# Attention ahead of two expert stages: keys and queries transposed head by head as loaded, with the sorting done while PSUM is emptied

## Chip, cores, metric

One core of one Trainium2 chip runs the whole program. The metric is the device time of one execution in microseconds; the kernel before took 967.55 us (median of three runs, 962.85 to 968.58).

## What is computed

The reference runs three stages in turn. Chunked attention: 8 batches, 8 heads, 576 positions, head width 64; each chunk of 64 positions attends to itself alone. Its output is read as 4608 rows (tokens) of 512 for two mixture-of-experts stages, each with 8 experts of which a row uses one.

```python
q_c = q.reshape(B, H, nc, chunk, D)                     # likewise k_c, v_c; chunk = 64
scores = scale * np.matmul(q_c, k_c.transpose(0, 1, 2, 4, 3))
scores = scores - np.max(scores, axis=-1, keepdims=True)
attn = np.exp(scores)
attn = attn / (np.sum(attn, axis=-1, keepdims=True) + 1e-09)
out = np.matmul(attn, v_c)                              # -> x of 4608 x 512
logits = x @ w_gate + modality_bias[modality_id]        # first expert stage; the second is alike
e_idx = np.argmax(logits, axis=1)
out[mask] = gate_w[mask, None] * (np.maximum(x[mask] @ w1[e], 0.0) @ w2[e])
```

## The kernel before

The attention runs over 36 tiles of 128 tokens. Two tiles are a unit: 256 tokens of all 8 heads, whose keys and queries are loaded together (`load_qk`, L434 to L443). Partition p of a loaded buffer holds the tokens 2p and 2p + 1 of each head, so that a run in memory is 512 bytes; heads lie outermost, then the token's parity r, then the 64 columns.

`reorder` (L452 to L460) copies such a buffer so that parity is outermost and two heads stand side by side. Units 0 to 2 are reordered by VectorE, units 3 to 17 by GpSimd, at L742 to L744. `emit_T` (L462 to L482) then makes one piece: four TensorE transposes of 128x128, for two head pairs and two parities, into one PSUM bank (tile `ps_t`, three buffers, shared with `ps_x`). A query piece is emptied by one ScalarE copy of 128x512 into `Tq` (L475), which puts even and odd tokens back in order by writing every second column. A key piece is emptied by two copies of 64x512 (L479), one for each head of the pairs, into `kb`, where the other head's half is blank so that one product serves two heads. A unit has four pieces (`pieces`, L484): keys and queries of the first two head pairs in its even slot, those of the last two in its odd slot.

The loop at L727 runs over the tiles; one turn t is a slot. Every engine works through its own queue in the order in which the slot names the work. TensorE's order is: scores of tile t + 2 (`emit_sc`, L497), first piece (keys, unit t // 2 + 2), transposes of the probabilities of tile t + 1 (`emit_pT`, L523), in each fourth slot the gate's products for four tiles (`emit_lg1`, L563), transposes of the output rows of tile t - 1 (`emit_xT`, L557), second piece (queries), products with the values of tile t (`emit_av`, L532). ScalarE empties the first piece, then `pt` (L525), in each fourth slot `lsb` (L567), `xT` (L558), the second piece, and runs exp for tile t + 2 (L515). VectorE takes the maximum and the difference of the scores (L506, L509) and normalises the output (L542 to L548).

Between these steps `drip()` calls one further step of `route` (L569), which chooses the expert of each row from the gate's products: small VectorE operations, the rank products (`ranks_mm`, L251 to L255), then four scatters into a table in device memory from GpSimd (L603). `wait2` is the number of calls that it lets pass ahead of the rank products. Three calls lie between the scores and the first piece.

Loads of keys, queries and values, stores and table blankings are all issued by SP, in program order. The table blankings are `tables` (L167), called from the list `g.late`, of which each slot takes three entries: in slot 2. From slot 20 on, `jobs` load the weights of the largest expert and split them (L637, L640). After the last tile the expert stages follow, which the change does not touch.

Of the kernel before, what the change touches and what calls it, by code (L numbers as in the profile page):

```python
# [134 lines left out]
def setup_late(nc, g, tmp, modality_id, modality_bias, w_gate2, w_skip):  # L135

    NT, NTILE, DM = g.NT, g.NTILE, g.DM
    md = tmp.tile([NTILE, P, 2], I32, name="md")
    nc.gpsimd.dma_start(
        out=md, in_=modality_id.bitcast(I32).rearrange("(t p w) -> t p w", p=P, w=2)  # L140
    )
    b01 = tmp.tile([P, 2, E], F32, name="b01")
    nc.gpsimd.dma_start(
        out=b01.rearrange("p m e -> p (m e)"),
        in_=modality_bias.rearrange("m e -> (m e)").unsqueeze(0).to_broadcast([P, 2 * E]),
    )
    wsm = tmp.tile([P, 4, E + 1], F32, name="wsm")
    nc.gpsimd.dma_start(out=wsm[:, :, 0:E], in_=w_gate2.rearrange("(a p) e -> p a e", p=P))
    nc.gpsimd.dma_start(
        out=wsm[:, :, E:E + 1], in_=w_skip.rearrange("(a p o) -> p a o", p=P, o=1)  # L150
    )


    blank = tmp.tile([P, g.NR // P, 2], I32, name="blank")
    nc.gpsimd.memset(blank[:, :, 0], int(OOB))
    nc.gpsimd.memset(blank[:, :, 1], 0)


    n = g.NR // P
    m = next(i for i in range(10, 0, -1) if n % i == 0)  # L160
    blank0 = tmp.tile([P, n // m, 16], I32, name="blank0")
    nc.gpsimd.memset(blank0, 0)
    nc.gpsimd.memset(blank0[:, :, 0], int(OOB))
    for t in g.row4:
        nc.gpsimd.memset(t, 0)

    def tables():  # L167
        nc.sync.dma_start(
            out=g.tab[0].rearrange("(p m n) c -> p m (n c)", p=P, m=m),
            in_=blank0.rearrange("p n c -> p (n c)").unsqueeze(1).to_broadcast([P, m, n // m * 16]),  # L170
        )
        nc.sync.dma_start(out=g.tab[1].rearrange("(p n) c -> p n c", p=P), in_=blank)

    nop = lambda: None

    mf = tmp.tile([NTILE, P], F32, name="mf")

    def bias():
        pm = g.ps_l.tile([P, P], F32, tag="l", name="pm")
        nc.tensor.transpose(pm[:, 0:NTILE], mf, g.ident[0:NTILE, 0:NTILE])  # L180
        m = tmp.tile([P, NTILE, 2], F32, name="m")
        nc.vector.tensor_copy(m[:, :, 1], pm[:, 0:NTILE])
        nc.vector.tensor_scalar(
            out=m[:, :, 0], in0=m[:, :, 1], scalar1=-1.0, scalar2=1.0, op0=ALU.mult, op1=ALU.add
        )
        t0 = tmp.tile([P, NTILE, E], F32, name="t0")
        sh = [P, NTILE, E]
        for i, dst in ((0, t0), (1, g.bias)):
            nc.vector.tensor_tensor(
                out=dst,  # L190
                in0=m[:, :, i:i + 1].to_broadcast(sh),
                in1=b01[:, i:i + 1, :].to_broadcast(sh),
                op=ALU.mult,
            )
        nc.vector.tensor_tensor(out=g.bias, in0=g.bias, in1=t0, op=ALU.add)

    def rows():

        pr = g.ps_l.tile([P, DM], F32, tag="l", name="pr")
        for a in range(4):  # L200
            nc.tensor.transpose(pr[0:E + 1, a * P:(a + 1) * P], wsm[:, a, :], g.ident)
        rw = tmp.tile([E + 1, DM], F32, name="rw")
        nc.scalar.copy(rw, pr[0:E + 1, :])
        nc.scalar.dma_start(out=g.rows, in_=rw)

    g.late = [lambda: nc.vector.tensor_copy(mf, md[:, :, 0])] + g.late + [tables, nop, bias, nop, nop, nop, rows]


def gate_argmax(nc, g, pool, lg, n, gate_out, comp=None):
# [178 lines left out]
def attention(ctx, tc, g, q, k, v, w_gate, w1, out, small):  # L388
# [11 lines left out]
    scale = 1.0 / float(D) ** 0.5  # L400
    ident = g.ident

    raw_p = ctx.enter_context(tc.tile_pool(name="raw", bufs=2))
    re_p = ctx.enter_context(tc.tile_pool(name="re", bufs=2))
    qt_p = ctx.enter_context(tc.tile_pool(name="qt", bufs=2))
    st_p = ctx.enter_context(tc.tile_pool(name="st", bufs=1))
    v_p = ctx.enter_context(tc.tile_pool(name="vp", bufs=1))
# [11 lines left out]
    kb = [v_p.tile([P, NA, 2, 4 * CH], F32, name=f"kb{i}") for i in range(2)]  # L419
    wg = g.const.tile([P, NA, 32], F32, name="wg")  # L420
    stage = [st_p.tile([P, 1024], F32, name=f"stage{i}") for i in range(2)]
    zero = g.zero[:, 0:1].unsqueeze(2).unsqueeze(3).to_broadcast([P, H, 2, D])

    def runs(t0, n):
        done = 0
# [3 lines left out]
            yield done, step, b, s  # L429
            done += step  # L430

    raw, re, T_ = {}, {}, {}

    def load_qk(u, queues=(nc.sync, nc.sync), parts=1):  # L434
        for src, nm, queue in ((k, "k", queues[0]), (q, "q", queues[1])):
# [13 lines left out]
            in_=v[b, h, c0 * CH:c1 * CH, :].rearrange("(c s) d -> s c d", s=CH),  # L449
        )  # L450

    def reorder(u, nm, eng, hs=slice(0, H)):  # L452
        t = raw[nm, u]
        if hs.start == 0:
            re[nm, u] = re_p.tile([P, 2, H, D], F32, tag="r" + nm, name="r" + nm)
        t2 = re[nm, u].rearrange("p r h d -> p h r d")
        if eng is nc.vector:
            eng.tensor_copy(t2[:, hs], t[:, hs])
        else:
            eng.tensor_tensor(out=t2, in0=t, in1=zero, op=ALU.add)  # L460

    def emit_T(u, nm, ah):  # L462
        t = re[nm, u]
        ps = ps_t.tile([P, 2, 2, P], F32, tag="t", name="ps_t")
        for a in range(2):
            for r in range(2):
                h = 2 * (2 * ah + a)
                nc.tensor.transpose(  # L468
                    ps[:, a, r, :], t[:, r, h:h + 2, :].rearrange("p h d -> p (h d)"), ident
                )  # L470
        sl = slice(2 * ah, 2 * ah + 2)
        if nm == "q":
            if ah == 0:
                T_[u] = qt_p.tile([P, NA, 4 * CH], F32, tag="Tq", name="Tq")
            nc.scalar.copy(T_[u][:, sl, :].rearrange("p a (c r) -> p a r c", r=2), ps)  # L475
        else:
            for j in range(2):
                eng = nc.vector.tensor_copy if u == 0 and j == 1 else nc.scalar.copy
                eng(  # L479
                    kb[u % 2][64 * j:64 * j + 64, sl, j, :].rearrange("p a (c r) -> p a r c", r=2),  # L480
                    ps[64 * j:64 * j + 64],
                )  # L482

    def pieces(u):  # L484
        return [lambda nm=nm, ah=ah: emit_T(u, nm, ah) for ah in range(2) for nm in ("k", "q")]
# [80 lines left out]
            )  # L566
        nc.scalar.copy(g.lsb, ps)  # L567

    def route(gi, wait=3, wait2=1):  # L569
        for _ in range(wait):  # L570
            yield
        ps = ps_l.tile([P, 4, NA, 32], F32, tag="l", name="ps_l2")
# [124 lines left out]
    ps = ps_t.tile([P, NA, P], F32, tag="t", name="ps_w")  # L697
    for i in range(15):
        nc.tensor.transpose(ps[:, i % NA, :], ident, ident)
    for i in range(2):  # L700
        for nm in "kq":
            reorder(0, nm, nc.vector, slice(i * H // 2, (i + 1) * H // 2))
    for f in pieces(0):
        f()
    reorder(1, "k", nc.vector)
    reorder(1, "q", nc.vector)
    T = pieces(1)
    emit_sc(0)
    emit_softmax(0)
# [11 lines left out]
    nc.gpsimd.dma_start(out=wg[:, :, 0:E], in_=w_gate.rearrange("(a p) e -> p a e", p=P))  # L721
    setup_late(nc, g, st_p, *small)
    load_qk(3)
    reorder(2, "k", nc.vector)
    reorder(2, "q", nc.vector)
    vq = []
    for t in range(NTILE):  # L727
        u = t // 2
# [8 lines left out]
        if t % 2 == 0:  # L737
            if u + 4 < NU:
                load_qk(u + 4)
            if u + 2 < NU:  # L740
                T = pieces(u + 2)
            for nm in "kq":  # L742
                if u + 3 < NU:
                    reorder(u + 3, nm, nc.gpsimd)  # L744
        if t >= 5 and (t - 5) % 4 == 0:
            store((t - 5) // 4)
        if t == NTILE - 3:
            nc.sync.dma_start(
                out=g.v0[:, 0:(E + 1) * DM],
                in_=g.rows.rearrange("e d -> (e d)").unsqueeze(0).to_broadcast([P, (E + 1) * DM]),  # L750
            )
# [738 lines left out]
```

## Time and profile before

| | us |
|---|---|
| median of three runs | 967.55 |
| lowest, highest | 962.85, 968.58 |
| the profiled execution | 963.45 |
| its span, first to last instruction | 961.8 |
| mean granted TensorE clock over the span | 0.985 |
| TensorE busy (matmuls) | 916.2 |
| VectorE, ScalarE, GpSimd busy | 648.6, 364.1, 321.8 |
| attention, to the end of its last product | 197.15 |

The profile is of one execution. A time in a timeline is counted from the span's start. A duration in a row is that of one instruction from its start to its end; where instructions overlap in an engine's pipeline, the next may start before that. In brackets stands how long the engine was idle before an instruction and what ended that.

### The profile page before, as it was taken

The numbers are of one execution on the slowest core, as the hardware profiler recorded it, in microseconds if no ns is written. First come the engines' busy times: TensorE is split into PE (matmuls) and PEld (weight loads), VectorE is DVE, ScalarE is ACT, GpSimd is POOL, SyncE is SP. The second block draws the span as 40 slices with busy tenths as digits, with TensorE's granted clock in tenths as the row PEclk, the third lists the DMA queues.
The fourth block names the chain that finished last, engine by engine and source line by source line (L and its number), as shares of the span: only waits on it lengthen the run. The fifth ranks groups of instructions, "written<-read, shape, count | busy, mean of one in ns | idle before, by whom it ended". The sixth has DMA issues, their size and how long they took to land. (4 is left out here: it accounts for less than half of the span.)

```text
span 961.8 us, 19826 instructions
## 1 busy us (share of the span) xinstructions
PE 916.2 (95%) x6757; PEld 812.0 (84%) x6757; DVE 648.6 (67%) x1853; ACT 364.1 (38%) x643; POOL 321.8 (33%) x288
## 2 busy tenths in 40 slices
PE   7889898999999999999999999999989997999996
PEld 6668777789999999989789999989879996998995
DVE  6567777678777777997887787787266265625261
ACT  5767686742222222522512222233145154515150
POOL 6447556434232323232232224212313121313310
PEclk9999998999999999999999999999999999999998
DMA  9999999757111111331111117000645366512400
GB/s 191 234 264 269 226 239 200 222 183 244 45 47 47 57 46 47 121 119 54 36 48 52 52 46 255 27 24 23 221 136 207 122 215 217 189 46 88 170 18 17
DMA packets 123292, 121.73 MB, mean 127 GB/s; under 512 B 55757, under 2 KB 94525, under 8 KB 122946
## 3 DMA queue, kind: packets, MB, share of 16 engines
q1 hardware_dynamic: 107536, 84.29, 32.5%
q0 software_dynamic: 14464, 34.43, 10.7%
q8 instruction: 83, 1.36, 0.7%
q14 instruction: 135, 1.11, 0.4%
q10 hardware_dynamic: 1074, 0.54, 0.2%
HBM read 96.37 MB, written 28.72 MB: 130 GB/s over the span
## 5 line engine op out<-in xcount | busy, mean ns | idle before, releaser
L1131 PE MATMUL p<-w2s,hT 128*128 128x512 f32 x1392 | 327.0, 392 | 0.2 <-DVEq L1246 0.2
L1131 PEld LDWEIGHTS p<-w2s,hT 128*128 128x128 f32 x1392 | 257.6, 188 | 51.5 <-DVEq L1246 0.6
L379 PE MATMUL p<-xTb,w1s 128*128 128x256 f32 x2064 | 262.0, 286 | 6.4 <-DVE hT L1096 3.0
L379 PEld LDWEIGHTS p<-xTb,w1s 128*128 128x128 f32 x2064 | 254.6, 192 | 11.1 <-DVE hT L1096 3.4
L1044 DVE CUSTOM_DVE_ANT_0 x<-x,v 128x512 f32<-128x512 f32 x333 | 210.5, 687 | 40.1 <-ACT x L1027 33.9
L1034 POOL DMA_INDIRECT out_dram<-x,ids x54 | 74.4, 1377 | 251.4 <-DVE x L1030 187.0
L1095 ACT ACTIVATE hT<-p 128x512 fp32r<-128x512 f32 x86 | 51.5, 599 | 194.6 <-PE p L379 169.9
L283 POOL DMA_INDIRECT tab<-rowP,posi x38 | 39.3, 1033 | 221.3 <-DVE idsP L1154 159.2
L1096 DVE SCALAR_TENSOR_TENSOR hT<-p,hT 128x512 fp32r<-128x512 f32 x86 | 58.9, 688 | 67.3 <-ACT hT L1095 44.7
L379 PE MATMUL p1t<-xTb,w1s 128*128 128x256 f32 x696 | 88.1, 283 | 0.0
L379 PEld LDWEIGHTS p1t<-xTb,w1s 128*128 128x128 f32 x696 | 85.1, 191 | 0.8 <-issue 0.8
L349 POOL DMA_INDIRECT x<-out_dram,ids x66 | 73.0, 1106 | 36.9 <-issue 17.3
L1027 ACT ACTIVATE x<-p,ids 128x512 f32<-128x512 f32 x33 | 22.7, 688 | 138.4 <-PE p L1131 130.8
L479 ACT COPY kb<-ps_t 64x512 f32<-64x512 f32 x70 | 43.9, 627 | 45.7 <-PE ps_t L468 45.3
L603 POOL DMA_INDIRECT tab<-row,posi x36 | 36.9, 1025 | 49.9 <-DVE x L548 24.2
L365 DVE TENSOR_TENSOR xTb<-px,xTb 128x512 fp32r<-128x512 f32 x70 | 44.8, 682 | 12.0 <-ACT xTb L364 12.0
L1004 DVE TENSOR_TENSOR w2s<-r,w2s 128x512 fp32r<-128x512 f32 x80 | 51.1, 688 | 1.2 <-ACT w2s L1002 0.8
L1002 ACT CAST w2s<-r 128x512 fp32r<-128x512 f32 x80 | 46.5, 625 | 8.1 <-issue 6.1
L364 ACT CAST xTb<-px 128x512 fp32r<-128x512 f32 x70 | 37.4, 591 | 27.6 <-PE px L362 27.6
L497 PE MATMUL sc<-kb,Tq 128*64 128x128 f32 x576 | 41.3, 284 | 5.8 <-DVE r_d L218 2.9
L1030 DVE SCALAR_TENSOR_TENSOR x<-p,ids,x 128x512 f32<-128x512 f32 x21 | 15.7, 749 | 44.2 <-PE p L1131 44.2
L497 PEld LDWEIGHTS sc<-kb,Tq 128*64 128x64 f32 x576 | 33.1, 141 | 10.4 <-issue 4.2
(229 smaller groups left out, 1102.4 us busy)
## 6 DMA issues: line engine op xcount, KB each, us to landing
r<-in_moe_w_dram SPq DMA_DIRECT2D x14, 2048.0 KB, 11.0
r<-in_moe_w_dram SPq DMA_DIRECT2D x20, 512.0 KB, 5.3
out_dram<-x SPq DMA_DIRECT2D x9, 1024.0 KB, 7.3
k<-in_k_dram SPq DMA_DIRECT2D x11, 512.0 KB, 6.4
q<-in_q_dram SPq DMA_DIRECT2D x11, 512.0 KB, 8.5
vt<-in_v_dram SPq DMA_DIRECT2D x32, 144.0 KB, 6.2
r<-in_moe_w_dram POOLq DMA_DIRECT2D x2, 2048.0 KB
v<-in_v_dram SPq DMA_DIRECT2D x24, 144.0 KB, 6.4
```

Of the source, the lines that this page charges most:

```text
L349: return [nc.gpsimd.indirect_dma_start(out=x[:, h, :], out_offset=None, in_=src, in_offset=IOff(ap=ids[:, h, 0:1], axis=0), bounds_check=s ...
L365: nc.vector.tensor_tensor(out=t[:, 1, :, h * P:(h + 1) * P], in0=ps, in1=o.bitcast(F32), op=ALU.subtract)
L379: nc.tensor.matmul(ps, w1s[:, b, kk, f * P:(f + 1) * P], xt[:, a, kk, :], start=(i == 0), stop=(i == 3 * KD - 1),)
L479: eng(kb[u % 2][64 * j:64 * j + 64, sl, j, :].rearrange("p a (c r) -> p a r c", r=2), ps[64 * j:64 * j + 64],)
L497: nc.tensor.matmul(out=ps[64 * c:64 * c + 64, a, :, :], lhsT=T_[u][:, a, cs], rhs=kb[u % 2][:, a, :, cs], start=True, stop=True,)
L1002: hi(s[:, 0, kk, :], r[:, kk, :])
L1004: eng.tensor_tensor(out=s[:, 1, kk, :], in0=r[:, kk, :], in1=s[:, 0, kk, :].bitcast(F32), op=ALU.subtract)
L1034: b = nc.gpsimd.indirect_dma_start(out=out, out_offset=IOff(ap=ids[:, h, 0:1], axis=0), in_=o[:, h, :], in_offset=None, bounds_check=NT - ...
L1044: nc.vector.tensor_tensor_reduce(out=junk[i % 2], in0=x2[:, h, :], in1=w2g[:, i, :], scale=1.0, scalar=0.0, op0=ALU.mult, op1=ALU.add, acc ...
L1095: nc.scalar.activation(out=o, in_=ps, func=AF.Relu)
L1096: nc.vector.scalar_tensor_tensor(out=l, in0=ps, scalar=0.0, in1=o.bitcast(F32), op0=ALU.max, op1=ALU.subtract)
L1131: nc.tensor.matmul(ps, hT[:, a, f, h * P:(h + 1) * P], w2s[:, b, f, :], start=(f == 0 and i == 0), stop=(f == KF - 1 and i == 2),)
```

## The change

`reorder` and its buffers go; the raw buffers become four instead of two. The transposes read the loaded buffer: one transpose takes one head with both its parities, so that in PSUM partitions 0 to 63 hold the even tokens and 64 to 127 the odd ones. Each piece is emptied by four copies of 64x256, one for each head and parity, all on one engine: VectorE for the queries of the last two head pairs, and in units 0 and 1 for the keys of the last two head pairs as well; ScalarE for the rest. Two of the four copies read one half of the partitions and write the other.

The blanking of the first table is cut into five DMAs, in slots 2 to 6; that of the second table moves to slot 20. `wait2` becomes 2.

```diff
-    def tables():
+    def table0(i, k):
+        a, b = i * m // k, (i + 1) * m // k
         nc.sync.dma_start(
-            out=g.tab[0].rearrange("(p m n) c -> p m (n c)", p=P, m=m),
-            in_=blank0.rearrange("p n c -> p (n c)").unsqueeze(1).to_broadcast([P, m, n // m * 16]),
+            out=g.tab[0].rearrange("(p m n) c -> p m (n c)", p=P, m=m)[:, a:b],
+            in_=blank0.rearrange("p n c -> p (n c)").unsqueeze(1).to_broadcast([P, b - a, n // m * 16]),
         )
-        nc.sync.dma_start(out=g.tab[1].rearrange("(p n) c -> p n c", p=P), in_=blank)
+    g.blanks = {t: (lambda i=i: table0(i, 5)) for i, t in enumerate(range(2, 7))}
+    g.blanks[20] = lambda: nc.sync.dma_start(out=g.tab[1].rearrange("(p n) c -> p n c", p=P), in_=blank)
...
-    raw_p = ctx.enter_context(tc.tile_pool(name="raw", bufs=2))
-    re_p = ctx.enter_context(tc.tile_pool(name="re", bufs=2))
+    raw_p = ctx.enter_context(tc.tile_pool(name="raw", bufs=4))
...
     def emit_T(u, nm, ah):
-        t = re[nm, u]
+        t = raw[nm, u]
         ps = ps_t.tile([P, 2, 2, P], F32, tag="t", name="ps_t")
         for a in range(2):
-            for r in range(2):
-                h = 2 * (2 * ah + a)
-                nc.tensor.transpose(
-                    ps[:, a, r, :], t[:, r, h:h + 2, :].rearrange("p h d -> p (h d)"), ident
-                )
+            for j in range(2):
+                h = 2 * (2 * ah + a) + j
+                nc.tensor.transpose(ps[:, a, j, :], t[:, h, :, :].rearrange("p r d -> p (r d)"), ident)
         sl = slice(2 * ah, 2 * ah + 2)
-            nc.scalar.copy(T_[u][:, sl, :].rearrange("p a (c r) -> p a r c", r=2), ps)
...
+        copy = nc.vector.tensor_copy if ah == 1 and (nm == "q" or u < 2) else nc.scalar.copy
+        for j in range(2):
+            d = slice(64 * j, 64 * j + 64)
+            o = T_[u][d, sl, :] if nm == "q" else kb[u % 2][d, sl, j, :]
             for r in range(2):
+                copy(o.rearrange("p a (c r) -> p a r c", r=2)[:, :, r, :], ps[64 * r:64 * r + 64, :, j, :])
...
-    def route(gi, wait=3, wait2=1):
+    def route(gi, wait=3, wait2=2):
...
-            for nm in "kq":
-                if u + 3 < NU:
-                    reorder(u + 3, nm, nc.gpsimd)
...
+        if t in g.blanks:
+            g.blanks[t]()
```

The calls of `reorder` for units 0 to 2 ahead of the loop go too, and `tables` in `g.late` becomes an empty entry.

## Rows read from the trace of the kernel before

**Rows 1.** The page, part 2: busy tenths of TensorE in 40 equal slices.

```profile
PE   7889898999999999999999999999989997999996
```

**Rows 2.** Windows: bounds, length, busy (instructions) PE, PEld, DVE, ACT, POOL; clock, DMA, GB/s.

```profile
21.83:32.98 11.15, 8.13 (x97) 6.91 (x96) 5.90 (x17) 7.07 (x13) 3.78 (x2) 1.00 1.04 204
32.98:66.80 33.82, 31.98 (x376) 25.84 (x376) 24.08 (x60) 25.13 (x46) 12.80 (x9) 1.00 1.12 266
66.80:80.92 14.12, 10.82 (x115) 9.23 (x114) 8.65 (x20) 6.39 (x13) 10.41 (x8) 0.88 1.11 255
80.92:180.81 99.89, 91.76 (x1091) 76.57 (x1090) 72.40 (x189) 75.17 (x135) 62.18 (x49) 0.97 1.00 225
180.81:197.15 16.34, 16.15 (x182) 13.05 (x182) 9.64 (x31) 8.52 (x17) 4.17 (x5) 1.00 0.79 273
```

**Rows 3.** TensorE's waits, 18 to 197 us: in total, times, longest.

```profile
PE ps_r L251 <- DVE r_oh L233: 4.2, 3, 3.4
```

**Rows 4.** Timeline of TensorE, 99 to 123 us: start, duration, instruction.

```profile
99.08 0.60 PE L523 MATMUL ps_p<-ident,e 128*128 128x128 f32 x4
...
99.95 0.60 PE L468 MATMUL ps_t<-ident,rq 128*128 128x128 f32 x4
...
101.43 0.60 PE L497 MATMUL sc<-kb,Tq 128*64 128x128 f32 x8
102.22 0.66 PE L497 MATMUL sc<-kb,Tq 128*64 128x128 f32 x8 [0.19 <-ACT Tq L475]
102.81 0.66 PE L468 MATMUL ps_t<-ident,rk 128*128 128x128 f32 x4
...
107.11 0.60 PE L523 MATMUL ps_p<-ident,e 128*128 128x128 f32 x4
...
112.31 0.66 PE L468 MATMUL ps_t<-ident,rk 128*128 128x128 f32 x4
...
116.76 1.09 PE L497 MATMUL sc<-kb,Tq 128*64 128x128 f32 x16 [1.44 <-DVE r_d L218]
...
122.36 0.66 PE L468 MATMUL ps_t<-ident,rk 128*128 128x128 f32 x4
```

**Rows 5.** Timeline of ScalarE, 105 to 115 us.

```profile
105.28 0.59 ACT L558 COPY xT<-ps_x 128x512 f32<-128x512 f32 x1
105.75 0.66 ACT L475 COPY Tq<-ps_t 128x512 f32<-128x512 f32 x1
106.28 0.65 ACT L515 ACTIVATE e<-e 128x512 f32<-128x512 f32 x1
...
113.01 1.27 ACT L479 COPY kb<-ps_t 64x512 f32<-64x512 f32 x2 [1.68 <-PE ps_t L468]
```

**Rows 6.** Groups of ScalarE by form, 20 to 197 us: count, busy, mean ns, idle before.

```profile
L479 ACT COPY kb<-ps_t 64x512 f32<-64x512 f32 x64 | 40.1, 627 | 40.2 <-PE ps_t L468 39.8
L515 ACT ACTIVATE e<-e 128x512 f32<-128x512 f32 x34 | 22.0, 646 | 1.9 <-DVE e L509 1.8
...
L226 ACT ACTIVATE r_ex<-r_d 128x32 f32<-128x32 f32 x8 | 1.8, 229 | 3.4 <-DVE r_d L218 3.4
```

**Rows 7.** Timelines of VectorE and GpSimd, 112 to 116 us.

```profile
112.18 3.03 DVE L581 TENSOR_TENSOR lgt<-lgt,bias 128x32 f32<-128x32 f32 x1
...
113.25 1.91 POOL L460 TENSOR_TENSOR rq<-q,zero 128x1024 f32<-128x1024 f32 x1
```

**Rows 8.** Timeline of all engines, 30 to 33 us: GpSimd and TensorE.

```profile
30.45 1.89 POOL L460 TENSOR_TENSOR rq<-q,zero 128x1024 f32<-128x1024 f32 x1 [0.67 <-DMA q<-in_q_dram]
...
32.40 0.66 PE L468 MATMUL ps_t<-ident,rq 128*128 128x128 f32 x4 [1.03 <-POOL rq L460]
```

**Rows 9.** Timeline of VectorE, 9 to 12 us.

```profile
9.54 1.30 DVE L479 COPY kb<-ps_t 64x512 f32<-64x512 f32 x2
```

**Rows 10.** Timelines of SP's queue, 41 us, and TensorE, 70 us.

```profile
41.62 3.24 SPq L172 DMA_DIRECT2D tab<-blank  x1
...
69.87 0.44 PE L532 MATMUL o_ps<-v,pt 128*64 128x130 f32 x4 [2.40 <-DMA v<-in_v_dram]
```

More of the change, by code (lines that the diff above doesn't have):

```diff
@@ L204, in rows @@
         nc.scalar.dma_start(out=g.rows, in_=rw)
-    g.late = [lambda: nc.vector.tensor_copy(mf, md[:, :, 0])] + g.late + [tables, nop, bias, nop, nop, nop, rows]
+    g.late = [lambda: nc.vector.tensor_copy(mf, md[:, :, 0])] + g.late + [nop, nop, bias, nop, nop, nop, rows]
 def gate_argmax(nc, g, pool, lg, n, gate_out, comp=None):
@@ L430, in runs @@
             done += step
-    raw, re, T_ = {}, {}, {}
+    raw, T_ = {}, {}
     def load_qk(u, queues=(nc.sync, nc.sync), parts=1):
@@ L450, in load_v, with emit_T @@
         )
-    def reorder(u, nm, eng, hs=slice(0, H)):
+    def emit_T(u, nm, ah):
         t = raw[nm, u]
[L454 to L462, printed above, removed]
-        t = re[nm, u]
         ps = ps_t.tile([P, 2, 2, P], F32, tag="t", name="ps_t")
         for a in range(2):
-            for r in range(2):
-                h = 2 * (2 * ah + a)
-                nc.tensor.transpose(
-                    ps[:, a, r, :], t[:, r, h:h + 2, :].rearrange("p h d -> p (h d)"), ident
-                )
[L471 to L474, printed above, removed]
-            nc.scalar.copy(T_[u][:, sl, :].rearrange("p a (c r) -> p a r c", r=2), ps)
[L476 to L482, printed above, removed]
+            for j in range(2):
+                h = 2 * (2 * ah + a) + j
+                nc.tensor.transpose(ps[:, a, j, :], t[:, h, :, :].rearrange("p r d -> p (r d)"), ident)
+        sl = slice(2 * ah, 2 * ah + 2)
+        if nm == "q" and ah == 0:
+            T_[u] = qt_p.tile([P, NA, 4 * CH], F32, tag="Tq", name="Tq")
+        copy = nc.vector.tensor_copy if ah == 1 and (nm == "q" or u < 2) else nc.scalar.copy
+        for j in range(2):
+            d = slice(64 * j, 64 * j + 64)
+            o = T_[u][d, sl, :] if nm == "q" else kb[u % 2][d, sl, j, :]
+            for r in range(2):
+                copy(o.rearrange("p a (c r) -> p a r c", r=2)[:, :, r, :], ps[64 * r:64 * r + 64, :, j, :])
     def pieces(u):
@@ L699, in attention @@
         nc.tensor.transpose(ps[:, i % NA, :], ident, ident)
-    for i in range(2):
-        for nm in "kq":
-            reorder(0, nm, nc.vector, slice(i * H // 2, (i + 1) * H // 2))
     for f in pieces(0):
         f()
-    reorder(1, "k", nc.vector)
-    reorder(1, "q", nc.vector)
     T = pieces(1)
@@ L723, in attention @@
     load_qk(3)
-    reorder(2, "k", nc.vector)
-    reorder(2, "q", nc.vector)
     vq = []
@@ L741, in attention @@
                 T = pieces(u + 2)
-            for nm in "kq":
-                if u + 3 < NU:
-                    reorder(u + 3, nm, nc.gpsimd)
         if t >= 5 and (t - 5) % 4 == 0:
             store((t - 5) // 4)
+        if t in g.blanks:
+            g.blanks[t]()
         if t == NTILE - 3:
```

1 line of the change is left out of this document (removed).

## The prediction

> **What bounds the kernel now.** I read the page first, for the stage in which each engine is full. TensorE's busy slices after the eighth of forty (192 us) are nearly all nines [rows 1]: the expert stages behind the attention wait for TensorE alone, so a microsecond won or lost in the attention moves the end by the same amount. The change touches only the attention, which ends at 197.15 us.
>
> Next the windows, cut where the product with the values (L532, "av") of tiles 0, 2, 9, 11 and 31 begins and where the last one ends [rows 2]. TensorE stands idle for 3.0 us in the first window, 1.8 in the second, 3.3 in the third and 8.1 in the fourth; in the third and fourth the granted clock is also below 1 (0.88 and 0.97, a mean of stretches at 2.4 and at 1.2 GHz). The longest wait is 3.4 us for `r_oh`, a VectorE step [rows 3]; the next, for values not yet loaded, comes below.
>
> The timeline then gives the pace. Four tiles, from the first key transposes (L468) at 102.81 to those at 122.36, take 19.55 us, of which 1.44 is a wait for VectorE [rows 4]. Without stalls it would be about 17.9. TensorE sets this pace; ScalarE, which empties the PSUM banks, comes just behind: from the first piece of an even tile (102.81) TensorE needs 4.30 us to the probability transposes of the next tile (L523, 107.11), which need ScalarE's exp. By that time ScalarE has done its own list: 0.70 from the transposes' start (112.31) to its first copy (113.01), two `kb` copies 1.30 to the next, `xT` and `pt`, of one form, 0.48 each, `Tq` 0.52, exp 0.65, and 0.05 back: 4.18 us [rows 4 to 6]. A cover of 0.12 us is all there is.
>
> **The change, part by part.** *Reordering gone.* The 30 GpSimd passes of 1.9 us (units 3 to 17, keys and queries) leave. Their own time is hidden, but while one runs, VectorE stands: an addition of 128x32 (`lgt`, L581) took 3.03 us, to 115.21, and GpSimd's `rq` pass ended at 115.16 [rows 7]. This is where TensorE's 1.44 us at 116.76 [rows 4] and the 3.4 us for `r_oh` [rows 3] come from. I count every stall of the fourth window as gone: 99.89 us for twenty tiles would become 5 x 17.9 = 89.5.
>
> At the start the transposes need not wait for the reordering: `rq` of the unit for tiles 6 and 7 began at 30.45 when its load landed, and TensorE's transposes waited until 32.40 [rows 8]. Straight from the load they start at 30.5, so av of tile 2 moves from 32.98 to about 31.0. Before that, transposes start a microsecond sooner but are followed by more copies; I take nothing, with 0.6 us either way.
>
> *The copies.* Per unit of two tiles, four `kb` copies of 64x512 and two `Tq` copies of 128x512 become sixteen of 64x256: the keys' eight and the first four of the queries' on ScalarE, the last four on VectorE. No row has this form. Below, the 128x32 form takes 0.23 us; above, 64x512 takes 0.627 [rows 6]. On the straight line between them 256 columns come to 0.415. Two `kb` copies take 1.27 us together, so a 64-partition copy does not overlap its follower, while `xT` of 0.59 is followed after 0.47 [rows 5]. I take 0.43 from one to the next.
>
> In an even tile ScalarE then does eight copies (3.44), `pt` and `xT` (0.96) and exp (0.65): 5.05 us instead of 3.43. Exp is queued last, so TensorE's L523 of the odd tile can start 0.70 + 5.05 + 0.05 = 5.80 us after the first key transposes, not 4.30. Cover gone, TensorE waits some 1.5 us once per unit, and behind that wait in its queue stand the `xT` and query transposes, av and the next scores, so VectorE's normalisation waits too.
>
> From L523 to the next unit TensorE needs 5.20 us with the gate's products in the tile (107.11 to 112.31) and 3.73 without (99.08 to 102.81), of which about 0.40 is a wait for `Tq` [rows 4]. That `Tq` now comes from VectorE: two 64x512 copies took 1.30 us there [rows 9]; half the size, about 0.34 each (between 0.1 and 0.65). Four after the transposes at 99.95 are ready 2.2 us later, when the second half of the scores would want them at 1.95: a wait of 0.25, so 3.57. A unit takes 5.80 + 5.20 = 11.00 or 5.80 + 3.57 = 9.37 us, four tiles **20.37**, against 19.55 to 20 before. VectorE's 1.4 us of copies per unit fit into its idle time (72 of 99.89 us busy [rows 2]).
>
> The ScalarE price is weighed against a rule. The Trainium skill (ScalarE: Activation LUTs, What ACT_TABLE_LOAD costs) states 186 ns + 0.833 ns per element for an ACTIVATE with immediate operands and says that back-to-back ones overlap by about 93 ns. By that 256 columns cost 399 ns, 306 to the next; the eight copies would be 2.45 us and four tiles about 18.4. The 128-partition rows agree with the overlap, the 64-partition pair does not [rows 5], and the measured pair decides; the rule lives on as the first rival.
>
> *Tables.* One 2320 KB blanking of the first table becomes five DMAs on SP over tiles 2 to 6, and the second table (290 KB) moves to tile 20. All pass in SP's queue among key, query and value loads. The bytes before the late values shrink by 290 KB, about 1.1 us at the window's 266 GB/s [rows 2]; its issue had held SP for 3.24 us [rows 10]. The values that TensorE got at 69.87, after a wait of 2.40 [rows 10], stand behind these bytes, so I take 1.1 us: 68.8. The scatters that need the blanked table stand on GpSimd, whose queue no longer holds reorderings.
>
> *Four raw buffers* cost nothing: a load waits for transposes four tiles back. *Ranks a slot later*: the routing is called three times between the scores and the first piece on TensorE, and the rank products move from the second call to the third, so they stay in place there; only VectorE's sums slip behind the query copies. Nothing.
>
> **The sum.** Av of tile 2 at 31.0. Query copies, exp and the remainder of the unit bring the next unit to 30.5 + 0.70 + 1.72 + 0.65 + 0.05 + 3.57 = 37.2; two units (11.00, 9.37) to 57.6; 5.80 and 2.55 (L523 to av with the gate) to av of tile 9 at 65.9, before 66.80. There the values still bind, until 68.8 instead of 69.87; as before some 3.5 us later, 72.3, the next unit starts, and av of tile 11 follows 5.80 + 0.87 + 0.53 later at 79.5 (before 80.92: 1.4 us won). Twenty tiles at 20.37 per four: 101.85, and 1.0 for the four weight casts (L637) that now lie on a tight ScalarE: 182.4 instead of 180.81. The last tiles (16.34 us) have no pieces and stay. Net **+1.6 us**: the profiled execution ran 963.45 us (span 961.8), so 965.1. That execution is 4.1 us below the median of 967.55; carried to the median, **969**.
>
> **Rivals.**
> 1. *Cheaper copies, faster.* If 64x256 copies overlap their followers as `xT` does, 0.31 to the next, each unit is 0.96 shorter: tile 11 at 78.5, twenty tiles 5 x 18.45 + 1 = 93.3, tile 31 at 171.8, 9.0 us sooner: 958.5. At 0.23, TensorE's own pace (89.5 + 1 from 78.0) gives 12.3 us: 955. For it: every 128-partition pair overlaps; the Trainium skill's rule above knows no other case. Against: the `kb` pair [rows 5].
> 2. *Dearer copies, slower.* The place is the same eight copies ahead of exp; two of four now write the other half of the partitions, which no row shows. At the 64x512 price, 0.65, a unit grows by 1.76: 2.4 to tile 9, then eleven units 19.4: 990. It is slower by over 1% from about 0.52 per copy. Query copies on VectorE at 0.65 would add 1.7 us per four tiles, 8.5 in all, on top. Against: the duration follows the columns in [rows 6].
> 3. *The clock.* If the new waits made the granted clock fall in every unit, TensorE's steps behind L523 would take up to twice their time: 15 units by 1 to 2 us, 984 to 999. Against: the 1.44 us wait left it at 1.00; it fell with waits of 2.40 and 3.4 us [rows 3, 10].
> 4. *The change wins nothing early* because loads bind the first 70 us anyway: this is already in the sum; if the smaller blankings don't bring the values sooner, it costs 1.1 us: 970.
>
> **Chances.** My forecast with rival 4 (965 to 974) 0.57; rival 1 0.26; rival 2 0.11; rival 3 0.06. About 1% (9.7 us) is what a measurement of this kernel can tell from no change. Over 1% faster (under 957.9) is the cheaper part of rival 1: 0.16; over 1% slower (above 977.2) is rival 3 and most of rival 2: 0.15; within 1%: 0.69. The range reaches close to rival 1's cheap end and to about 0.52 per copy on the other side: **956 to 978**; the forecast's own range is 965 to 974.
>
> **What would show it.** Right: 64x256 ScalarE copies near 0.42 us with no overlap; one TensorE wait of 1 to 1.5 us per unit at L523, ended by ScalarE's exp; four tiles near 20.4 us between tiles 11 and 31; no VectorE step of 128x32 over 1 us except beside the L640 splits; av of tile 2 near 31; the clock at 1.00 but for the wait for values. Wrong: a wait at L523 that doesn't exist (rival 1), copies of 0.5 us or more (rival 2), a clock below 1 through the stage (rival 3), or TensorE's waits in the expert stages changing, which I hold to be untouched.

## The result, and the profile after

The changed kernel took 975.88 us (median of six runs, 970.23 to 978.24), the kernel before beside it 965.47 us (961.06 to 968.58). The ratio is **1.0107, 95% interval 1.0081 to 1.0132**: 10.4 us slower. The forecast was 969, the range 956 to 978, so the time lies inside the range, 6.9 us above the forecast, on the border between "within 1%" and "slower", and outside the 965 to 974 that the forecast itself had with a chance of 0.57. Its profiled execution ran 978.24 us with a span of 976.7 (before: 963.45 and 961.8); the attention ends at 206.54 us instead of 197.15.

Windows of the changed kernel, cut as in [rows 2] where the product with the values (now L521) of tiles 0, 2, 9, 11 and 31 begins and at the last one's end; same columns.

```profile
20.38:30.23 9.85, 8.06 (x98) 6.94 (x97) 6.88 (x21) 7.99 (x20) 0.00 (x0) 1.00 1.13 207
30.23:67.49 37.26, 32.55 (x377) 25.67 (x376) 25.33 (x73) 31.06 (x72) 0.00 (x0) 1.00 1.08 250
67.49:81.50 14.01, 10.88 (x115) 8.71 (x115) 7.28 (x24) 7.32 (x19) 4.23 (x5) 0.88 1.07 271
81.50:189.40 107.90, 92.77 (x1091) 75.33 (x1090) 76.13 (x229) 86.34 (x195) 29.13 (x31) 0.98 0.92 207
189.40:206.54 17.14, 16.35 (x182) 13.05 (x182) 11.50 (x35) 8.38 (x16) 4.20 (x5) 1.00 0.75 264
```

Tile 2 starts 2.75 us earlier than before, tile 9 0.7 later, tile 11 0.6 later, and the twenty tiles behind that take 8.0 us more. GpSimd's busy time there falls from 62.18 to 29.13 us and ScalarE's rises from 75.17 to 86.34. TensorE stands idle for 15.1 us in that stretch, where it was 8.1.

TensorE's waits, 18 to 207 us: in total, times, longest. The wait for `r_oh` of [rows 3] is gone.

```profile
PE ps_p L512 <- ACT e L504: 14.1, 15, 1.3
PE sc L486 <- DVE Tq L471: 6.3, 9, 1.0
PE sc L486 <- DVE e L498: 2.7, 3, 1.4
PE o_ps L521 <- DMA v<-in_v_dram: 2.3, 2, 1.2
PE sc L486 <- ACT w1s L626: 1.1, 1, 1.1
```

The pace, to be laid beside [rows 4]: timeline of TensorE over a unit without the gate.

```profile
95.38 0.66 PE L461 MATMUL ps_t<-ident,k 128*128 128x128 f32 x4
...
98.22 1.04 PE L486 MATMUL sc<-kb,Tq 128*64 128x128 f32 x16
...
99.56 0.64 PE L461 MATMUL ps_t<-ident,k 128*128 128x128 f32 x4
101.01 0.66 PE L512 MATMUL ps_p<-ident,e 128*128 128x128 f32 x4 [0.81 <-ACT e L504]
...
101.94 0.60 PE L461 MATMUL ps_t<-ident,q 128*128 128x128 f32 x4
...
103.42 0.60 PE L486 MATMUL sc<-kb,Tq 128*64 128x128 f32 x8
104.81 0.66 PE L486 MATMUL sc<-kb,Tq 128*64 128x128 f32 x8 [0.79 <-DVE Tq L471]
105.40 0.66 PE L461 MATMUL ps_t<-ident,k 128*128 128x128 f32 x4
```

Two waits to a unit of two tiles. The first is ScalarE's (its timeline, as in [rows 5]): exp comes last, behind eight copies.

```profile
96.08 1.65 ACT L471 COPY kb<-ps_t 64x256 f32<-64x256 f32 x4 [2.26 <-PE ps_t L461]
97.75 0.59 ACT L514 COPY pt<-ps_p 128x512 f32<-128x512 f32 x1
98.23 0.59 ACT L547 COPY xT<-ps_x 128x512 f32<-128x512 f32 x1
98.71 1.59 ACT L471 COPY Tq<-ps_t 64x256 f32<-64x256 f32 x4
100.33 0.63 ACT L504 ACTIVATE e<-e 128x512 f32<-128x512 f32 x1
100.87 0.21 ACT L230 ACTIVATE r_ex<-r_d 128x32 f32<-128x32 f32 x1
```

The second is VectorE's:

```profile
101.11 0.19 DVE L244 TENSOR_REDUCE r_sm<-r_ex 128x4 f32<-128x32 f32 x1 [1.54 <-ACT r_ex L230]
101.33 0.17 DVE L246 TENSOR_SCALAR r_sm<-r_sm 128x4 f32<-128x4 f32 x1
101.54 0.18 DVE L248 RECIPROCAL row<-r_sm 128x4 f32<-128x4 f32 x1
101.63 0.66 DVE L495 TENSOR_REDUCE mx<-sc 128x8 f32<-128x512 f32 x1
102.33 0.69 DVE L498 TENSOR_TENSOR e<-sc,mx 128x512 f32<-128x512 f32 x1
```

The scores were ready at 99.26, but `mx` begins at 101.63: at the head of VectorE's slot stands `r_sm`, a sum of the gate's routing, which needs ScalarE's `r_ex`, and `r_ex` was issued behind the copies and exp. Then follow `e` and the query copies, from 102.94, although their transposes had ended at 102.54.

Groups by form, attention only: count, busy us, mean ns, idle time before them.

```profile
L471 ACT COPY kb<-ps_t 64x256 f32<-64x256 f32 x128 | 51.2, 400 | 35.8 <-PE ps_t L461 33.7 <-PE ps_p L512 0.6
L471 DVE COPY Tq<-ps_t 64x256 f32<-64x256 f32 x64 | 27.5, 430 | 20.9 <-PE ps_t L461 20.2
L570 DVE TENSOR_TENSOR lgt<-lgt,bias 128x32 f32<-128x32 f32 x8 | 1.5, 188 | 0.2
```

The addition that took 3.03 us in [rows 7] has a mean of 0.188 us: VectorE's stalls beside GpSimd's sorting are gone. The values of tile 9, timeline of TensorE in the changed kernel:

```profile
69.34 0.44 PE L521 MATMUL o_ps<-v,pt 128*64 128x130 f32 x4 [1.19 <-DMA v<-in_v_dram]
70.89 0.61 PE L521 MATMUL o_ps<-v,pt 128*64 128x130 f32 x4 [1.10 <-DMA v<-in_v_dram]
```

and in the kernel before, where the wait of [rows 10] is followed by a second one:

```profile
70.90 0.44 PE L532 MATMUL o_ps<-v,pt 128*64 128x130 f32 x4 [0.59 <-DMA v<-in_v_dram]
```

### The profile page after: what moved, and what is told of

Read it like the earlier page. It is cut to its first block, busy times and chain, and to the rows that moved or that the text cites. A ratio compares the mean times of both kernels' runs of the same rounds, so it can differ in the third digit from the quotient of the medians.

```text
span 976.7 us, 19937 instructions
## 1 busy us (share of the span) xinstructions
PE 916.7 (94%) x6757; PEld 808.7 (83%) x6757; DVE 653.7 (67%) x1923; ACT 382.5 (39%) x745; POOL 265.7 (27%) x258
## 5 line engine op out<-in xcount | busy, mean ns | idle before, releaser
L471 ACT COPY kb<-ps_t 64x256 f32<-64x256 f32 x136 | 54.3, 399 | 40.2 <-PE ps_t L461 38.0
```

What stands on the lines that cost most here:

```text
L471: copy(o.rearrange("p a (c r) -> p a r c", r=2)[:, :, r, :], ps[64 * r:64 * r + 64, :, j, :])
```

## Experiments

All ratios are to the kernel before on the same chip. "Four tiles" is from tile 12's product with the values to tile 16's (before 19.56, changed 20.90 us); "rest" is the span less the end of the attention, the expert stages, which no edit touches. Where a slot is given a time, it runs from its tile's product with the values to the next tile's. The last five kernels ran on other chips than the first seven; what that does is told at e10_unsorted.

| kernel | median us | ratio, 95% interval | attention ends | four tiles | rest |
|---|---|---|---|---|---|
| changed | 975.88 | 1.0107, 1.0081 to 1.0132 | 206.5 | 20.90 | 770.2 |
| e2_exp_first | 969.53 | 1.0045, 1.0024 to 1.0067 | 200.8 | 19.51 | 767.2 |
| e3_sum_later | 971.44 | 1.0083, 1.0052 to 1.0114 | 203.5 | 20.56 | 765.1 |
| e4_whole_tables | 974.68 | 1.0110, 1.0073 to 1.0147 | 204.1 | 20.88 | 768.2 |
| e5_half_heads | 970.35 | 1.0059, 1.0041 to 1.0076 | 201.8 | 21.22 | 767.1 |
| e6_exp_first_sum_late | 968.04 | 1.0024, 0.9999 to 1.0049 | 202.3 | 18.55 | 765.3 |
| e7_gpsimd_adds_back | 985.88 | 1.0213, 1.0176 to 1.0250 | 213.8 | 21.27 | 771.8 |
| e8_ranks_early | 975.18 | 1.0105, 1.0070 to 1.0139 | 205.0 | 20.97 | 770.8 |
| e9_all_three | 975.07 | 1.0065, 1.0044 to 1.0087 | 205.1 | 20.74 | 765.5 |
| e10_unsorted | 967.59 | 0.9982, 0.9964 to 0.9999 | 199.0 | 19.23 | 764.6 |
| e11_rows_later | 980.33 | 1.0115, 1.0089 to 1.0140 | 210.2 | 21.69 | 765.3 |
| e12_queues_loads_casts | 972.95 | 1.0034, 1.0016 to 1.0051 | 208.8 | 19.83 | 764.6 |
| e13_before_loads_casts | 971.39 | 1.0004, 0.9981 to 1.0028 | 205.8 | 19.71 | 767.4 |

**Exp ahead of the second piece.**

```diff
+        if t + 2 < NTILE:
+            emit_exp(t + 2)
         piece()
-        if t + 2 < NTILE:
-            emit_exp(t + 2)
```

> Changed kernel with one line moved: the exp of tile t+2 is issued ahead of the second piece, so that on ScalarE it no longer stands behind the four query copies. The theory (TensorE waits 14.1 us in all, 15 times, at L512 for an exp that stands behind the copies) expects that row to shrink under 3 us and the end of attention to come 6 to 12 us earlier, total 964 to 970 us. Rival, ScalarE is simply full in even slots: the wait only moves to the scores or to the next key copies, gain under 2 us, total 974 to 977.

The wait at L512 is gone altogether, four tiles take 1.4 us less, the attention ends 5.7 us sooner (6 at least was expected), and the ratio falls by 0.0062, 6.0 us. What is left of TensorE's waits is VectorE's chain, now bare (same view as above):

```profile
PE sc L486 <- DVE e L498: 7.6, 8, 1.8
PE sc L486 <- DVE Tq L471: 7.1, 9, 1.0
```

The wait for `e` had 2.7 us in the changed kernel: TensorE comes earlier to the scores and finds VectorE still behind `r_sm`. So the position of one line was more than half of the loss, and a second wait stood partly hidden behind the first.

**The routing's sum later.**

```diff
-    yield
+    for _ in range(1 if comp is not None else 3):
+        yield
     sm = pool.tile([P, n], F32, tag="r_sm", name="r_sm")
...
-    def route(gi, wait=3, wait2=2):
+    def route(gi, wait=3, wait2=0):
```

> Changed kernel with r_sm, its +1e-9 and its reciprocal two steps later (behind e instead of at the head of VectorE's slot), and the ranks where they are now. The theory (in slots 4k+3 r_sm waits up to 1.6 us for r_ex, which stands on ScalarE behind the copies and exp; mx, e, the VectorE query copies and so TensorE's scores come late behind it: 6.3 us in 9 waits) expects VectorE's wait for r_ex to go and the waits of the scores for Tq to fall from 0.8 to under 0.5 each, total 970 to 973.5 us. Rival, the VectorE copies alone (1.73 us for four) make the wait: the waits for Tq stay at 0.8, total 975 to 977.

Two steps turned out to be too few: `r_sm` itself still stands ahead of `mx` (it waited 1.53 us for `r_ex`, then ran at 99.39 with `mx` at 99.49), and only its two followers moved behind. VectorE's wait for `r_ex` stays, 7.7 us against 9.1; the waits for `Tq` in slots 11, 15 and 19 fall from 0.86, 0.79 and 0.83 to 0.52, 0.46 and 0.51. The ratio falls by 0.0024, 2.3 us, which the two intervals can't tell from nothing; in the profiles the attention ends 3.0 us sooner. The time lies in the range expected; the mechanism came in half.

**Both, with the sum four steps later.**

```diff
+    for _ in range(1 if comp is not None else 5):
+        yield
...
+    def route(gi, wait=3, wait2=0):
...
+        if t + 2 < NTILE:
+            emit_exp(t + 2)
         piece()
```

> Changed kernel with exp ahead of the second piece, and r_sm, its +1e-9 and its reciprocal four steps later, so that they stand behind e on VectorE (ranks two steps later too). The theory (two queues in order make the loss: exp behind the query copies on ScalarE; mx, e and the VectorE query copies behind r_sm, which waits for r_ex on ScalarE) expects that moving exp alone leaves the second wait bare, and that both together give more than the sum of each alone less one: no wait for e over 0.4 us, lap 18.3 to 18.9 us, total 962 to 967 us. Rival, the four VectorE query copies (1.73 us) hold the scores back by themselves: scores still wait 0.6 us or more for Tq in slots 4k+3, lap 19.2 us or more, total 968 to 971.

Four tiles take 18.55 us, 2.35 less than in the changed kernel and 1.0 less than before. That is more than the two gains together (1.39 and 0.34 us), also because the sum now stands behind `e`. Yet the ratio falls only by 0.0083, 8.0 us, to that of the kernel before within the error, and the median misses the 962 to 967 us expected by 1 us. Three slots give it back: 9, 23 and 27 took 11.19, 9.87 and 10.11 us, where their like take about 4.5. Slot 23 on VectorE and TensorE:

```profile
137.59 0.69 DVE L630 TENSOR_TENSOR w1s<-stage,w1s 128x512 fp32r<-128x512 f32 x1 [1.96 <-ACT w1s L627]
...
140.20 1.00 PE L487 MATMUL sc<-kb,Tq 128*64 128x128 f32 x8 [2.09 <-DVE e L499]
...
144.17 1.06 PE L513 MATMUL ps_p<-ident,e 128*128 128x128 f32 x4
```

The weight's subtraction waits on VectorE for ScalarE's cast, `mx` and `e` of the attention wait behind it, and after TensorE's 2.09 us the granted clock is 0.67 over the slot: the transposes take 1.06 us instead of 0.66.

**Whole tables, and the ranks as before.** The first puts `tables` back, the second is `wait2=1`.

> Changed kernel with the tables blanked as in the kernel before (two whole DMAs in one early slot), all else as changed. The theory (the parts change nothing that lasts) expects the wait of av(9) for values to stay at about 2.3 us and the total within 2 us of the changed kernel, 974 to 978. Rival A, the parts cost the loss by standing ahead of values and keys on SyncE's queue: 966 to 971. Rival B, the parts do gain what they are put there for: 979 to 982.

> Changed kernel with the ranks one step earlier, as in the kernel before (wait2=1). The theory (TensorE waited up to 3.4 us for r_oh only because VectorE was stalled beside GpSimd; without that the later slot does nothing) expects no wait of the rank products over 0.3 us and the total within 2 us of the changed kernel, 974 to 978. Rival A, the later slot is a gain that remains: 979 to 983. Rival B, the later slot is part of the loss: 970 to 973.

Neither moves the time (974.68 and 975.18 against 975.88). In e4 the wait for the values of tile 9 is gone, other than expected: the attention ends 2.4 us sooner, which the medians can't tell apart. In e8 the rank products wait once, 0.5 us, where at most 0.3 was expected.

**GpSimd's additions back.**

```diff
+    def reorder(u, nm):
+        t = raw[nm, u]
+        nc.gpsimd.tensor_tensor(out=t, in0=t, in1=zero, op=ALU.add)
...
+            for nm in "kq":
+                if u + 3 < NU:
+                    reorder(u + 3, nm)
```

> Changed kernel with GpSimd's two 128x1024 additions of zero put back in each even slot, in place on the loaded keys and queries, where the sorting copies were; values are unchanged. They are the sorting copies' work without the sort, so they size the term that the change took away. The theory (what was gained is VectorE's stalls while GpSimd holds the ports) expects small VectorE operations of 0.19 us to grow to about 1 us again where they lie beside an addition, and the total 4 to 12 us above the changed kernel: 979 to 988. Rival, those stalls never lay on the path that sets the end: within 2 us of the changed kernel, 973 to 978.

About 10 us slower (985.88; the ratio rises by 0.0106), as expected: this is what such additions cost the changed kernel. In the profiles tile 11 starts 3.5 us later than in the changed kernel (84.95 against 81.50), and the twenty tiles behind it take 3.8 us more (111.72 against 107.90). VectorE, GpSimd and TensorE in slot 10:

```profile
76.29 4.43 DVE L225 SCALAR_TENSOR_TENSOR r_er<-r_d,rev 128x32 f32<-128x32 f32 x1
...
76.89 1.92 POOL L458 TENSOR_TENSOR k<-k,zero 128x1024 f32<-128x1024 f32 x1
78.75 1.91 POOL L458 TENSOR_TENSOR q<-q,zero 128x1024 f32<-128x1024 f32 x1
...
81.22 0.20 PE L255 MATMUL ps_r<-r_oh,upper 128*128 128x8 bf16 x2 [2.79 <-DVE r_oh L237]
```

An operation of 0.19 us lasts until GpSimd's second addition has ended, and behind TensorE's wait of 2.79 us the granted clock falls: 0.80 over the slot, which takes 8.51 us. The Trainium skill (GPSIMD Engine Reference, 1. Specifications) says that GpSimd's SBUF interfaces are shared with VectorE, with contention for VectorE's operations that run in a 2-port mode or have two SBUF inputs. The trace agrees: `r_d` and `rev` are two SBUF inputs.

Not every VectorE operation stands still. VectorE and GpSimd in the kernel before:

```profile
106.30 0.69 DVE L548 TENSOR_TENSOR x<-o_ps,rs 128x512 f32<-128x512 f32 x1
...
105.77 1.90 POOL L460 TENSOR_TENSOR rq<-q,zero 128x1024 f32<-128x1024 f32 x1
```

`x`, with one input in PSUM, starts 0.53 us into an addition and takes 0.69 us as without one, and `e` and `mx` keep their times too. In that trace `lgt`, `r_d` and the product of `r_z` and `r_oh` (two SBUF inputs) and the cast to `posi` (one) grow, from 0.12 to 0.19 us to between 0.93 and 4.56.

**No sorting copies at all.**

```diff
+            for r in range(2):
+                for j in range(2):
+                    h = 2 * (2 * ah + a) + j
+                    nc.tensor.matmul(out=ps[64 * j:64 * j + 64, a, r, :], lhsT=t[:, h, r, :], rhs=ident, start=True, stop=True)
...
+            nc.scalar.copy(T_[u][:, sl, :].rearrange("p a (c r) -> p a r c", r=2), ps)
```

> Changed kernel without any sorting copy: each transpose takes one row parity of one head (128x64 stationary out of the loaded tile, 64 output partitions), eight of them to a piece in place of four, so that the PSUM tile has the order of the kernel before; emptied by that kernel's copies (one 128x512 ScalarE copy for queries, two 64x512 for keys). Raw buffers, tables and ranks as changed. The theory (the 64x256 copies and what stands behind them are the loss; the sorting copies that are gone are a gain) expects no wait of TensorE for exp over 0.3 us, none for Tq, no long 128x32 operation on VectorE, laps of four tiles of 17.8 to 19.0 us (20.9 in the changed kernel, 19.9 in the one before), end of attention at 186 to 191 us, total 954 to 961 us. Rival A, TensorE pays for eight small transposes (a piece 1.0 us or more in place of 0.6): lap over 20 us, total 966 to 975. Rival B, the loss isn't in the copies: total 972 to 977.

The copies' waits go, as the theory has it; the price is rival A's. From tile 11 to tile 31 TensorE never stands idle, at full clock (windows, as above), and still needs 106.09 us:

```profile
79.84:185.93 106.09, 106.09 (x1574) 91.60 (x1572) 60.76 (x188) 76.18 (x136) 29.64 (x31) 1.00 0.91 213
```

```profile
94.86 1.09 PE L461 MATMUL ps_t<-ident,q 128*64 128x128 f32 x16
```

A piece of eight small products with the identity leaves sixteen records and lasts 1.09 us, four transposes leave four and last 0.60. Rival A was right, and TensorE's work has replaced its waits.

**The copies alone, unsorted.**

```diff
-                copy(o.rearrange("p a (c r) -> p a r c", r=2)[:, :, r, :], ps[64 * r:64 * r + 64, :, j, :])
+            nc.scalar.copy(T_[u][:, sl, :].rearrange("p a (c r) -> p a r c", r=2), ps)
```

> Changed kernel with its transposes head by head, but emptied by the copies of the kernel before (one 128x512 on ScalarE for queries, two 64x512 for keys): work is left out, keys and queries come out unsorted, so the output isn't the reference's, and since other rows choose other experts only the attention's part of the time can be compared. It sizes the copies alone. The theory expects no wait of TensorE at L512 over 0.3 us and none for Tq over 0.3, four tiles in 17.8 to 18.6 us (20.9 with the sorting copies), end of attention at 185 to 190 us against 206.5. Rival, the copies are half of the loss at most and tables, ranks or the casts the rest: four tiles in 19.5 us or more, end of attention at 195 us or later.

The ratio can't be set beside the changed kernel's, since other rows choose other experts; in the attention the copies are worth 7.6 us (199.0 against 206.5), with what is said of the chips below. The slots without the gate are as expected, 4.16 and 4.22 us (changed: 5.2 and 4.8). The slots with the gate are not: 5.7 and 5.3 us instead of the 4.96 and 4.55 of the kernel before. So four tiles take 19.23, between the two forecasts, and the attention ends at 199.0, in the rival's range; waits for `Tq` of up to 1.2 us stay (2.5 in all), where none over 0.3 was expected. VectorE and GpSimd in slot 16, where TensorE's product with the values ended at 101.67 and the scores at 102.54:

```profile
103.94 0.17 DVE L534 TENSOR_SCALAR rs<-o_ps 128x8 f32<-128x8 f32 x1 [3.75 <-PE ps_p L515]
...
105.49 0.69 DVE L498 TENSOR_REDUCE mx<-sc 128x8 f32<-128x512 f32 x1 [0.41 <-PE ps_l L555]
...
103.36 0.97 POOL L595 DMA_INDIRECT tab<-row,posi  x1 [0.30 <-issue]
```

and the same place in e6_exp_first_sum_late, product ended at 105.46:

```profile
105.51 0.17 DVE L532 TENSOR_SCALAR rs<-o_ps 128x8 f32<-128x8 f32 x1 [0.59 <-PE o_ps L522]
...
106.94 0.97 POOL L593 DMA_INDIRECT tab<-row,posi  x1 [0.30 <-issue]
```

In both, GpSimd issues its four scatters about the product: the first starts 1.0 us ahead of it in e10 and with it in e6. In the second VectorE follows the product after 0.05 us, in the first after 2.3. e11 (below) has the program of the changed kernel but for the place of one DMA: behind the products of tiles 9, 12, 16 and 20, beside the scatters, VectorE follows after 1.2 to 2.3 us, in the changed kernel after 0.03 to 0.05. TensorE's wait for `lsb` is 1.4 to 4.7 us in all in the five kernels on these chips and at most 0.7 in the others, and the kernel before has a median of 969.5 there, 964 to 965.5 on the first ones. So absolute times of the two groups can't be set side by side, and the gate's slots of the second group carry something that the changed kernel's own profile doesn't.

**The values, and a combined version.** The first moves the DMA of `rows` from slot 4 to slot 12, because the row of waits of SyncE (SP) in the changed kernel reads

```profile
SPq L449 <- DMA rows<-rw: 5.4, 1, 5.4
```

which holds the value loads of slot 5. The blankings have a part in it: the kernel before has no such row, and e4, with whole tables, has

```profile
SPq L446 <- DMA rows<-rw: 1.1, 1, 1.1
```

The others put it together with e6, with value loads four to a slot and with casts and subtractions in slots of their own; the last makes the same three moves in the kernel before.

```diff
+    g.late = [lambda: nc.vector.tensor_copy(mf, md[:, :, 0])] + g.late + [nop, nop, bias, nop, nop, nop] + 24 * [nop] + [rows]
...
-        for _ in range(2 if t >= 4 else 4):
+        for _ in range(4):
...
+            lambda: (load(0), load(1)), nop, lambda: cast(0), lambda: split(0), lambda: load(2), nop,
+            lambda: cast(1),
...
```

> Changed kernel with the DMA of `rows` in slot 12 instead of slot 4, all else as changed. My prediction had the values of tile 9 come 1.1 us sooner for the smaller blankings; they didn't. The theory (SyncE's value loads of slot 5 wait 5.4 us for that DMA, whatever the blankings) expects SyncE's wait for rows to go, no wait for values at tile 9 over 0.3 us, the clock at 1.00 there, tile 11 at 76 to 79 us instead of 81.5, and the total 2 to 5 us under the changed kernel, 971 to 974. Rival, the loads are late because the DMA engines are full up to there: the wait for values stays over 1 us and the total within 1.5 us, 974.5 to 977.5.

> Exp ahead of the second piece and r_sm behind e, as in e6_exp_first_sum_late, and two moves more. The DMA of `rows` (an entry of g.late, on ScalarE's queue) goes from slot 4 to slot 12: in the changed kernel and in e6, SyncE held the values' loads of slot 5 back for 5.4 to 6.2 us behind it. Of the four weight casts, each is followed by its VectorE and GpSimd subtractions one slot later, and the casts stand at the ends of even slots (22, 24, 26, 28). The theory (what e6 gains in its laps of 18.6 us is given back in slots 9, 23 and 27, which took 11.2, 9.9 and 10.1 us with waits of 2.7 to 4.0 us and TensorE at half clock behind them) expects no wait over 1 us in the attention, the clock at 0.97 or more in each slot from 9 to 31, the end of attention at 184 to 189 us and the total at 949 to 956, faster than both kernels. Rival, the waits in these slots come from elsewhere (the values' own DMA time, the weights' load): at least one of the slots stays over 8 us, total 960 to 967.

> e6_exp_first_sum_late with three moves: the DMA of `rows` in slot 12 instead of 4; values loaded four DMAs to a slot throughout, so that those of tile 9 are issued in slots 5 and 6, ahead of two units of keys and queries; the four weight casts in slots 22, 26, 30 and 32 and their subtractions a slot later. The theory (e6 loses some 6 us in slot 9 to late values and the half clock behind, and some 10 us in slots 23 and 27 to casts and subtractions in one slot) expects slot 9 under 6 us, no slot from 10 to 31 over 7 us, the clock at 0.98 or more in the attention, and 7 to 13 us less than the kernel before on the same chip, ratio 0.987 to 0.993. Rival, the loads as such are the limit of the first 70 us and the casts cost the same wherever they stand: ratio 0.998 to 1.006.

> The kernel before with the same three moves (rows, values, casts), its sorting copies and queues untouched. The theory (before loses some 5 us in slot 9 and some 4 us in slot 26 to the same late values and casts) expects 4 to 9 us less than before, ratio 0.991 to 0.996, and, since its laps stay at 19.5 to 20 us against 18.6, 2 to 6 us more than e12_queues_loads_casts. Rival, the stalls of VectorE beside GpSimd take up what the moves win: ratio 0.998 to 1.002.

In e11 the wait for values at tile 9 is gone, the clock there is 1.00 and tile 11 starts at 77.0 us, as expected; but the ratio stays at 1.0115. The twenty tiles from tile 11 on take 114.59 us instead of 107.90, so by the ratio the rival had the total right, but not the reason. In e9 the wait is longer than ever, 5.2 us in two: its tiles run ahead and reach tile 9 at 62.5, before the values can be there. Three slots stay over 8 us, as the rival has it, and the total is outside both ranges. In e12, with the loads issued earlier, slot 9 takes 4.88 us at full clock, and slots 23 and 27 take 5.3: these two parts of the theory held. But the slots with scatters grew, on VectorE and TensorE in slot 25:

```profile
153.94 1.73 DVE L472 COPY Tq<-ps_t 64x256 f32<-64x256 f32 x4 [4.33 <-remote]
...
155.82 1.12 PE L487 MATMUL sc<-kb,Tq 128*64 128x128 f32 x8 [3.31 <-DVE Tq L472]
```

The query transposes had ended by 151.0, the last scatter of the slot at 153.0. Slots 11, 17, 25 and 29 took 8.7 to 12.1 us with the clock at 0.72 to 0.82, and the total missed the forecast: 1.0034, in the rival's range. The same moves do nothing for the kernel before either (1.0004; its `r_oh` now waits 5.0 us once, in slot 10). **No version here that sorts the keys and queries beats the kernel before**; e6 and e13 equal it within the error. Whether e6 with its casts apart would beat it on the first chips was not tried.

## Why the prediction was right, and where it was mis-sized

*Stalls gone:* right. No VectorE operation of 128x32 is long but beside the weights' subtractions, and e7 shows that the additions cost the changed kernel time: about 10 us when they come back. My sum had credited the fourth window with 10.4 us (99.89 to 89.5). That the two are alike is luck: in that window e7 loses only 3.8 us, and TensorE's waits for exp there fall meanwhile from 8.7 to 6.5 us. And "while one runs, VectorE stands" was too broad, as the rows at e7 show.

*The copies' price:* right. 0.400 and 0.388 us each on ScalarE against 0.415, four in 1.65 and 1.59 us, so 0.41 apart against 0.43. Rivals 1 and 2 both fall with these rows. By the formula of the Trainium skill (ScalarE: Activation LUTs, What ACT_TABLE_LOAD costs) the duration is 399 ns, an estimate, and followers overlap by about 93 ns. The duration agrees; the overlap does not show in these 64-partition copies.

*One wait of TensorE per unit for exp:* right in place and count, 15 waits in the whole attention, nearly all of 0.8 to 1.3 us (the shortest 0.25) where I had 1.5. e2 takes it away, and 6.0 us with it.

*The query copies on VectorE:* this term was mis-sized. I had 0.34 each from half a 64x512 copy and counted from the end of their transposes, a wait of 0.25. They take 0.43, and they start 0.40 late, behind `r_sm`, which waits for ScalarE's `r_ex`. The wait is 0.79 to 0.86 in slots 11, 15 and 19. I had costed what stands behind exp on TensorE, but not that `r_ex` stands behind exp on ScalarE, and that VectorE's whole slot stands behind `r_ex`. e6 shows it: with this second wait moved too, four tiles take 18.55. A unit's way to exp came 0.17 short (95.38 to 101.01 is 5.63 instead of 5.80), the remainder of the unit without the gate 0.82 long (101.01 to 105.40 is 4.39 instead of 3.57). Four tiles came to 20.97 and 20.87 instead of 20.37: 5 x 0.53 = 2.7 us over tiles 11 to 31.

*The casts:* mis-sized too, 3.4 us (107.90 less 5 x 20.90) instead of 1.0, nearly all in slot 23 (7.75 us; TensorE waits 0.62 us for `e` and 1.05 behind the cast, and the clock falls to 0.81, where I had it at 1.00 but for the wait for values). Before, slot 26 lost as much (9.34 us at 0.75), so it is a loss that moved rather than one that came.

*The values:* wrong. I had them 1.1 us sooner for the smaller blankings. TensorE waits for them twice, before and after, and I had counted from the first wait only. The second ended at 70.90 before and at 70.89 after: nothing was won, because SyncE's loads of slot 5 stood 5.4 us behind the DMA of `rows`. The granted clock then fell to half at 71.0 us, where before it fell at 72.3, so the next key transposes came 3.49 us behind the values instead of 2.49. The 1.1 and this 1.0 make tile 11 start at 81.50 instead of 79.5. e4 and e11 take this wait away in two ways, and the median doesn't show it.

*The end:* the stretch from tile 31 on takes 17.14 instead of 16.34 us, one more wait for `Tq` (0.78).

These four make 2.7 + 2.4 + 2.0 + 0.8 = 7.9 us; the attention ended 9.4 us later, my sum had 1.6, and the two make 9.5.

*The number:* that it lies in the range is in part luck. The range reached up to 978 for ScalarE copies of 0.52 us, and these cost 0.40; the loss came from the four terms above, which had no room of their own in it. And the kernel before had 965.47 beside the changed one, not the 967.55 that I started from: as a difference I had 1.6 us, and 10.4 were measured.

*The expert stages untouched:* the code is, the time is not quite. The rest of the profiled execution took 770.2 us against 764.6. But the twelve other profiles in which rows choose the same experts lie between 764.6 and 771.8, in no order that follows the edits. The clock goes with it: leaving out the stretch in which each execution ends, the changed kernel's expert stages pass 23.9 us at half clock, before 13.7. The 10.2 us more would cost about 5.1 us, an estimate by half of that time. So a difference of 5.5 us there between two single executions is no effect of the change that could be shown; the medians' 10.4 us would be the attention's 9.4 and about one more, if the profiled attentions are typical. Why these stretches differ stays open.

## What to carry over

When work moves onto an engine, list everything that stands behind it in that engine's queue and not only the instruction that another engine waits for: here a 0.2 us exponential of the routing, two places further back, stopped a second engine's whole slot. Taking a wait away shows the next one, and in a kernel whose end is set by TensorE the order in two queues was worth nearly as much (8.0 us, e6) as the work that the change saves (about 10 us, e7). Behind a long wait, read the granted clock of the slots that follow as part of its price: slots 9, 23 and 27 of e6 waited 2.7 to 4.0 us and took 5 to 7 us more than their like.

## What the runs showed of the hardware

- ScalarE copies on 64 partitions follow each other without overlap: 64x256 takes 0.40 us and the next starts after 0.41, while the 128x512 copies of 0.59 are followed after 0.48. On VectorE 64x256 out of PSUM takes 0.43 us, more than the 0.34 that I had made of half a 64x512 copy.
- While a GpSimd addition runs, VectorE's operations with an input in PSUM keep their time (0.69 us for 128x512), and the small ones with two inputs in SBUF last until it has ended, or until the second of two in a row has (3.03 us before, 4.43 in e7, instead of 0.19).
- A float32 product with a 64-column stationary operand leaves two records, a transpose of 128x128 one: eight products with the identity cost 1.09 us, four transposes 0.60, for the same bytes.
- On the chips of the last five kernels VectorE often follows TensorE late while GpSimd issues indirect DMAs, by 2.3 us in slot 16 of e10_unsorted and by 2.9 in slot 25 of e12_queues_loads_casts; in the changed kernel and in e6 the same pattern costs nothing. What causes it, the runs don't show.
- Executions with the same expert stages differ there by up to 7 us (764.6 to 771.8).
